# One attention-and-adapters kernel: the last twenty-four slots follow an order written out by hand instead of a loop

## The chip, the core and the metric

The kernel runs on one core of one Trainium2 chip. The core has engines that each work through their own queue in order: TensorE (PE, matmuls, with its weight loads shown apart as PEld), VectorE (DVE), ScalarE (ACT), GpSimd (POOL), and SyncE (SP), which here only issues DMAs. An engine waits on semaphores that others raise, so one late instruction holds up all that stands behind it in its queue. The metric is the device time of one execution in microseconds (us), as the median of several runs.

## The reference

Two stages follow each other. The first is attention with keys and values made from a pooled map (`kv` is averaged over 4 x 4 blocks and multiplied by `w_sr`); the second routes each row to two of eight small adapters.

```python
# B, N, C = 4, 12288, 128; 768 pooled keys a batch
kv_flat = kv_pool.reshape(B, -1, C) @ w_sr        # k = v = kv_flat
s = scale * (q @ k.transpose(0, 2, 1))
a = np.exp(s - s.max(-1, keepdims=True)); a /= a.sum(-1, keepdims=True) + 1e-09
x = (a @ v).reshape(B * N, C)                     # 49152 rows
logits = x @ w_gate                               # 8 experts, the best 2 are kept
w = softmax of the two kept logits
out = x + sum over the two of w_e * ((x @ A[e]) @ B[e])   # A: 128 x 16, B: 16 x 128
```

## The kernel before

The rows are cut into 96 chunks of 512 (24 a batch). A chunk is four tiles of 128 rows. Its way through the core has these steps, each a function of the kernel; all matmuls are issued by the helper on line 68, so the profile tells them apart by their tiles:

- `scores(k, r)` for r = 0, 1, 2 (line 238): two matmuls of 512 columns into one of two PSUM tiles `sg` (pool `ps_s`), then ACT's exp into `em` (line 246). Six score matmuls and three exps a chunk.
- `attend(k, s)` for the four tiles s (line 248): six matmuls each into `acc`, of which PSUM holds one (`ps_a`). Columns 128 to 135 of the product are already the gate logits, column 136 the sum.
- `normalize` (line 256): reciprocal and multiplication on DVE, `acc` into `xn`.
- `top` (line 276): four MAX8 on DVE. `route` (line 285): four small steps on POOL that turn the two largest logits into a tanh argument and a mask. `gates` (line 310): the tanh on ACT and two more steps on POOL give the weights `gw`.
- `transposes(kx, kh)` (line 318): four transposes of one chunk's `xn` and four of an older chunk's gated values `hg` into one PSUM tile `tt_ps`, copied out by one instruction (line 334 on ACT, line 336 on DVE).
- `down` (line 342), four matmuls by A into `h_ps`; `gate` (line 347), the product with `gw` on DVE into `hg`; `up` (line 356), four matmuls by B into `d_ps`; `finish` (line 361), the addition of `xn` on DVE and the output DMA from SP.

The tiles `tt_ps`, `h_ps`, `d_ps` share a pool `ps_m` of two PSUM banks (tag `mb`). Together `sg`, `acc` and `mb` fill PSUM. Output tiles `osb` come from a pool of six (line 59). The queries are cast to bf16 by POOL's DMAs (`cast_q`, line 77) and read back transposed by SP's DMAs (`load_qT`, line 82), four chunks at a time; a one-column copy on POOL named `late` makes a cast wait for the transposed read of the group before it.

The order is the program's order: each engine gets its instructions as the Python code emits them. A loop over chunks (line 420, from chunk 4 on) emits one *slot* for each chunk k: score 0 of k, the normalisation of k-2, transposes for k-6 and k-7, score 1, `up` and `finish` of k-8, the first tile of attend k-1, `top` and `route`, score 2, `down` and `gate` of k-6, the other three tiles of attend k-1. Chunks are routed in pairs up to chunk 71 and one by one from 72 (line 269). Three slots let two chunks enter instead of one, so that the backlog shrinks from six chunks to three:

```python
can = [k for k in left if ready[k] <= t]
enter[t] = can[:2] if t in [NB * (B - 1) + 1 + i for i in (0,1,3)] else can[:1]
```

These are slots 73, 74 and 76; the second chunk's transposes are copied by ACT (line 334), and its `down` follows in the next slot. After the loop (line 500 on) the last four chunks are finished by straight code with its own helpers: single transposes copied by ACT (`fetch`, line 523), the last attention in an `sg` tile, a carried output (`carry`, line 561: ACT copies `d_ps` to SBUF; `add_there`, line 566: POOL adds `xn` there and SP sends it), and half-chunk steps at the very end (lines 573, 644, 558).

Of the kernel before, what the change touches and what calls it, by code (L numbers as in the profile page):

```python
# [20 lines left out]
def kernel(  # L21
# [85 lines left out]
    def turn_q(g, m, engine):  # L107
        if m == 0:
            qT[g] = qpool.tile([P, GT], BF16, tag="qT", name="qT")
        ps = mtile([P, S, P], name="qT_ps")  # L110
        for i in range(S):
            mm(ps[:, i], q_f[g][:, m * S + i], id_f, is_transpose=True,
               start=(i == 0), stop=(i == S - 1))
        o = qT[g][:, m * T:(m + 1) * T].rearrange("p (s t) -> p s t", s=S)
        if engine is nc.scalar:
            keep(nc.scalar.copy(o, ps))
        else:
            keep(nc.vector.tensor_copy(o, ps))
# [39 lines left out]
    def prepare(b, adder):  # L158
# [28 lines left out]
        def keys(h):  # L187
            if h == 0:
                st["kpT"] = prep.tile([P, J, P], FP32, tag="kpT", name="kpT")
                kfT[b] = per_b.tile([P, J, P], BF16, tag="kfT", name="kfT")  # L190
            kpT = st["kpT"]
            ps = mtile([P, 2, P], name="kpT_ps")
# [4 lines left out]
            for n, (r, i, c) in enumerate(parts):  # L197
                mm(ps[:, i], kvr[b, h][:, r, i, c * C:(c + 1) * C], id_f, is_transpose=True,
                   start=(n == 0), stop=(n == len(parts) - 1))
            keep(nc.vector.tensor_scalar(kpT[:, 2 * h:2 * h + 2], ps, 1.0 / 16.0, None,  # L200
# [27 lines left out]
        for h in range(3):  # L228
            for f in (keys, keys2, values) if adder is nc.vector else (keys, values, turn):
                rest.append(lambda h=h, f=f: f(h))  # L230
# [7 lines left out]
    def scores(k, r):  # L238
        b = k // NB
        if r == 0:  # L240
# [7 lines left out]
    def attend(k, s):  # L248
        b = k // NB
        if s == 0:  # L250
# [5 lines left out]
    def normalize(k):  # L256
        ri = rpool.tile([P, S], FP32, tag="rinv", name="rinv")
        keep(nc.vector.reciprocal(ri, acc[k][:, :, VC]))  # L258
        k0, m = first[k], k - first[k]
        if m == 0:  # L260
            xg[k0] = xpool.tile([P, GC, S, VC], FP32, tag="xn", name="xn")
        x = xg[k0][:, m]
# [13 lines left out]
    def top(k):  # L276
        k0, m = first[k], k - first[k]
        if m == 0:
# [4 lines left out]
    later = []  # L283

    def route(k0):
        n = size[k0] * S
        eng = nc.gpsimd if k0 > 1 else nc.vector
        lg = xg[k0].rearrange("p m s c -> p (m s) c")[:, 0:n, C:VC]
# [10 lines left out]
        keep(eng.tensor_scalar(mask, mask, 0.0, None, op0=ALU.is_ge))  # L299


        def rest():
            gates(k0, n, eng, arg, mask)

        if k0 > 3:
            later.append(rest)
        else:
            rest()

    def gates(k0, n, eng, arg, mask):  # L310
# [50 lines left out]
    def finish(k):  # L361
# [5 lines left out]
        for d in (em, acc, xn, xT, hgT, hp, hg, dp):  # L367
            d.pop(k, None)

    LA = 4  # L370

    for m in range(GC):
        turn_q(0, m, nc.scalar)
    sums, rest = prepare(0, nc.vector)
    for h in range(3):
        for item in sums[h]:
            item()
        rest[3 * h]()
        if h > 0:
            scores(2, h - 1)  # L380
        rest[3 * h + 1]()
        if h > 0:
            scores(3, h - 1)
            rest[3 * h - 1]()
        scores(0, h)
        scores(1, h)
    rest[8]()
    scores(2, 2)
    scores(3, 2)
    rest = []  # L390

    late = const.tile([P, 1], FP32)
    keep(nc.gpsimd.tensor_copy(late, q_f[1][:, GC * S - 1, 0:1]))
    for g in range(2, 4):
        cast_q(g)
    a_bf = const.tile([P, P], BF16)
    keep(nc.vector.tensor_scalar(a_bf, a_f, 0.5, None, op0=ALU.mult))
    b_bf = const.tile([P, C], BF16)
    keep(nc.vector.tensor_copy(b_bf, b_f))
    turn_q(1, 0, nc.scalar)  # L400


    att = {LA: [0], LA + 1: [1], LA + 2: [2, 3], LA + 3: [4, 5], LA + 4: [6, 7]}
    for k in range(8, NCHUNK):
        att[k + 1] = [k]
    normed = {}
    for t, ks in att.items():
        for k in ks:
            normed[k] = t + 1 if k == ks[-1] else t
    ready = {k: normed[first[k] + size[k] - 1] + 1 for k in range(NCHUNK)}  # L410
    enter, t, left = {}, LA, list(range(NCHUNK - 3))
    while left:
        can = [k for k in left if ready[k] <= t]
        enter[t] = can[:2] if t in [NB * (B - 1) + 1 + i for i in (0,1,3)] else can[:1]
        left = [k for k in left if k not in enter[t]]
        t += 1

    sums, rest = [], []
    kh, ku, kd, kdone = [], [], [], []
    for k in range(LA, NCHUNK):  # L420
        b, i = divmod(k, NB)
        ka = att.get(k, [])
        kx = enter.get(k, [])
        if k % GC == 0:
            g = k // GC
            if 2 <= g + 1 < B * NG:
                load_qT(g + 1)
        if b + 1 < B:
            i0 = 4 if b == 0 else 0
            if i == i0:  # L430
                sums, rest = prepare(b + 1, nc.gpsimd)
                sums = sum(sums, [])
            if i0 <= i < i0 + 12:
                h, j = divmod(i - i0, 4)
                load_kv(b + 1, h, j, None)

        if k % GC == 2 and 4 <= k // GC + 2 < B * NG:
            keep(nc.gpsimd.tensor_copy(late, qT[k // GC + 1][:, 0:1]))
            cast_q(k // GC + 2)

        def after_norm(kn):
            top(kn)
            if kn == first[kn] + size[kn] - 1:
                route(first[kn])

        kn = [n for n in att.get(k - 1, []) if normed[n] == k]
        if k == LA:
            for s in range(S):
                attend(0, s)
            ka = []  # L450
        scores(k, 0)
        while later:
            later.pop(0)()
        for x_ in kd:
            down(x_)
        for n in kn:
            normalize(n)
        pairs = [(kx[j] if j < len(kx) else None, kh[j] if j < len(kh) else None)
                 for j in range(max(len(kx), len(kh)))]
        for x_, h_ in pairs[:1]:  # L460
            transposes(x_, h_, nc.vector)
        for x_ in kd:
            gate(x_)
        if k + 1 in range(GC + 1, 2 * GC):
            turn_q(1, (k + 1) % GC, nc.scalar)
        scores(k, 1)
        for u_ in ku:
            up(u_)
            finish(u_)
        for a_ in ka[:-1]:  # L470
            for s in range(S):
                attend(a_, s)
            normalize(a_)
            after_norm(a_)
        if ka and len(ka) == 1:
            attend(ka[0], 0)
        for n in kn:
            after_norm(n)
        scores(k, 2)
        for x_ in kx[:1]:  # L480
            down(x_)
            gate(x_)
        kd = []
        if rest and i in ((14, 15, 16, 18, 19, 20, 21, 22, 23) if b == 0 else (11, 12, 13, 17, 18, 19, 21, 22, 23)):
            rest.pop(0)()
        for a_ in ka[-1:]:
            for s in range(1 if len(ka) == 1 else 0, S):
                if s == S - 1:
                    for x_, h_ in pairs[1:]:
                        transposes(x_, h_, nc.scalar)  # L490
                        kd = [x_] if x_ is not None else []
                attend(a_, s)
        ku = kh
        kh = kx[:1] + kdone
        kdone = kd
        if b + 1 < B and i % 2 == 0 and (8 if b == 0 else 6) <= i <= 20:
            for _ in range(4 if b == 0 and i % 4 else 3):
                sums.pop(0)()

    K = NCHUNK - 1  # L500
    assert kh == [K - 3] and ku == [K - 4], (kh, ku)

    def bank(pool):
        if pool is ps_m:
            return mtile([P, S, P], name="tail_ps")
        if pool is ps_a:
            return ps_a.tile([P, S, 256], FP32, tag="acc", name="acc")
        return ps_s.tile([P, 2, T], FP32, tag="sg", name="sg")

    def turn_x(k, pool):  # L510
        ps = bank(pool).bitcast(BF16).rearrange("p a b -> p (a b)")[:, 0:T].rearrange("p (s c) -> p s c", s=S)
        xb = xn[k].bitcast(U16)[:, :, 1::2].bitcast(BF16)
        for s in range(S):
            mm(ps[:, s], xb[:, s, 0:C], id_bf, is_transpose=True, start=(s == 0), stop=(s == S - 1))
        xT[k] = ps

    def turn_h(k, pool):
        ps = bank(pool).bitcast(BF16).rearrange("p a b -> p (a b)")[:, 0:T].rearrange("p (s c) -> p s c", s=S)
        for s in range(S):
            mm(ps[:, s], hg[k][:, s], id_bf, is_transpose=True, start=(s == 0), stop=(s == S - 1))  # L520
        hgT[k] = ps

    def fetch(which, k):
        sb = run.tile([P, S, P], BF16, tag="tt1", name="tt1")
        keep(nc.scalar.copy(sb, which[k]))
        which[k] = sb

    def tanhs():
        for rest_ in later:
            rest_()  # L530
        later.clear()

    def part(k, o, js):
        for s in range(S):
            for j in js:
                mm(o[:, s, 0:VE], em[k][:, j, s * P:(s + 1) * P], vx[k // NB][:, j],
                   start=(j == 0 and s % 2 == 0), stop=(j == J - 1 and s % 2 == 1))

    def wide(o):
# [148 lines left out]
```

## Time and profile before

| what | value |
|---|---|
| median of 5 runs | 400.67 us (399.65 to 401.01) |
| the profiled execution | 399.65 us, of which its span is 397.9 us |
| mean granted TensorE clock | 0.996 |
| PE busy | 374.2 us (94% of the span) |
| DVE, ACT, POOL busy | 324.5, 297.3, 202.0 us |
| first score matmul of chunk 72 | 292.42 us after the span's start |
| end of slot 95 (the loop) on PE | 385.38 us |
| last DVE instruction ends | 394.73 us |
| output DMA of 256 KB, issue to landing | 3.4 us median over the run |

The profile lists instructions by line, engine, operation and tiles, with `out<-in`. A record of a matmul includes its way through the array, so records overlap: what a matmul costs PE in a stream is the distance between the starts. "Idle before" is the time in which an engine waited just before an instruction, with what ended the wait.

### The profile page before, as it was taken

The page shows a single profiled execution, that of the slowest core. Times are in us where ns is not written, and L with a number is a line of the kernel's source. Part 1 is how long each engine was busy: PE and PEld are TensorE (multiplying, and loading weights), DVE is VectorE, ACT ScalarE, POOL GpSimd, SP SyncE. Part 2 cuts the span into 40 slices and gives each one's busy share as a digit, 9 for nine tenths or more (in the row PEclk, how much of TensorE's full clock was granted, in tenths as well). Part 3 has the DMA queues.
Part 4 walks back from the last instruction along what each step waited for, and adds up shares of the span by engine and source line. Part 5 has one row for each costly group of instructions (what it writes and reads, how often), then busy time and mean ns, then how long its engine had stood idle before and what let it go on. Part 6 is the DMA issues. An engine that isn't in the chain of part 4 may idle for free.

```text
span 397.9 us, 11637 instructions
## 1 busy us (share of the span) xinstructions
PE 374.2 (94%) x4515; PEld 302.3 (76%) x4589; DVE 324.5 (82%) x944; ACT 297.3 (75%) x375; POOL 202.0 (51%) x471
## 2 busy tenths in 40 slices
PE   4898899999999999999999999999999899999993
PEld 3656678788888887888878887888877688788882
DVE  2543778889898889898898888898888788888885
ACT  3389467877787787787777787786778778888873
POOL 0010159977623586876613486876614244344443
PEclk9999999999999999999999999999999999999998
DMA  8998637996588999955679999956644477464113
GB/s 291 402 248 244 157 110 207 265 251 158 130 205 227 287 235 348 186 153 132 145 167 265 243 255 276 282 139 138 150 135 106 133 187 159 135 144 123 62 74 135
DMA packets 71464, 76.47 MB, mean 192 GB/s; under 512 B 49936, under 2 KB 50704, under 8 KB 70928
## 3 DMA queue, kind: packets, MB, share of 16 engines
q1 hardware_dynamic: 70272, 63.98, 55.0%
q0 software_dynamic: 704, 11.54, 16.7%
q8 instruction: 36, 0.59, 0.6%
q10 hardware_dynamic: 432, 0.20, 0.2%
q14 instruction: 20, 0.16, 0.2%
HBM read 50.53 MB, written 36.70 MB: 219 GB/s over the span
## 4 chain that ended last, share of the span: by engine, by line
PE 81%; DVE 5%; POOL 4%; ACT 3%; DMA 3%; issue 2%; SPq 1%; ACTq 0%; DVEq 0%; POOLq 0%
PE acc L68 32%; PE sg L68 23%; PE tt_ps L68 10%; PE h_ps L68 6%; PE d_ps L68 6%; ACT em L246 2%; POOL kvr L171 2%; PE kpT_ps L68 1%; DMA qf<-in_q_dram 1%; DVE rinv L258 1%; DMA kvr<-in_kv_dram 1%; PE v_ps L68 1%; DVE xn L263 1%; SPq L98 1%; DVE tts L336 1%
## 5 line engine op out<-in xcount | busy, mean ns | idle before, releaser
L246 ACT ACTIVATE em<-sg 128x1024 f16<-128x1024 f32 x288 | 280.7, 1024 | 78.1 <-PE sg L68 59.0
L68 PE MATMUL acc<-vx,em 128*128 128x137 f16 x2280 | 167.5, 223 | 1.3 <-DVE xn L263 1.2
L68 PE MATMUL sg<-qT,kfT 128*128 128x512 bf16 x502 | 155.2, 379 | 3.1 <-ACT em L246 2.6
L68 PEld LDWEIGHTS <-em 128*128 128x128 f16 x2304 | 145.4, 98 | 3.2 <-DVE xn L263 2.2
L68 PEld LDWEIGHTS <-tts 128*128 128x128 bf16 x740 | 56.4, 98 | 46.1 <-issue 2.8
L263 DVE TENSOR_TENSOR xn<-acc,rinv 128x544 f32<-128x544 f32 x95 | 68.8, 724 | 3.4
L293 POOL TENSOR_TENSOR over<-xn,srt 128x64 f32<-128x64 f32 (+1 forms) x116 | 30.3, 282 | 80.0 <-DVE srt L281 80.0
L350 DVE TENSOR_TENSOR hg<-h_ps,gw 128x512 bf16<-128x512 f32 x93 | 64.3, 691 | 7.4 <-PE h_ps L68 0.2
L171 POOL TENSOR_TENSOR kvr<-kvr 128x512 f32<-128x512 f32 x54 | 67.3, 1270 | 0.0
L336 DVE COPY tts<-tt_ps 128x1024 bf16<-128x1024 bf16 (+1 forms) x90 | 62.0, 689 | 1.7 <-PE tt_ps L68 0.9
L363 DVE TENSOR_TENSOR osb<-d_ps,xn 128x512 f32<-128x512 f32 x91 | 62.6, 691 | 0.6 <-PE d_ps L68 0.6
L68 PEld LDWEIGHTS <-kfT 128*128 128x128 bf16 x576 | 45.8, 98 | 6.7 <-issue 4.3
L314 POOL TENSOR_TENSOR gw<-th,over 128x64 f32<-128x64 f32 (+1 forms) x58 | 16.9, 292 | 66.6 <-ACT th L312 66.3
L258 DVE RECIPROCAL rinv<-acc 128x4 f32<-128x4 f32 x95 | 17.4, 183 | 35.4 <-PE acc L68 35.1
L68 PEld LDWEIGHTS <-xn 128*128 128x128 bf16 x384 | 29.1, 98 | 20.9 <-DVE xn L263 0.4
L68 PE MATMUL h_ps<-a_bf,tts 128*128 128x128 bf16 x372 | 36.0, 219 | 2.0 <-ACT tts L334 0.7
L68 PE MATMUL d_ps<-b_bf,tts 128*128 128x128 bf16 x364 | 35.2, 219 | 2.7 <-DVE tts L336 1.1
L68 PE MATMUL tt_ps<-id_bf,xn 128*128 128x128 bf16 x372 | 35.9, 219 | 1.2
L68 PE MATMUL tt_ps<-id_bf,hg 128*128 128x128 bf16 x368 | 35.6, 219 | 0.3 <-DVE hg L350 0.3
L281 DVE MAX8 srt<-xn 128x8 f32<-128x8 f32 x380 | 34.2, 153 | 0.2
L68 PEld LDWEIGHTS <-hg 128*128 128x128 bf16 x384 | 25.6, 98 | 1.3 <-DVE hg L350 0.5
L299 POOL TENSOR_SCALAR over<-over 128x64 f32<-128x64 f32 (+1 forms) x58 | 19.4, 335 | 5.2
(82 smaller groups left out, 201.4 us busy)
## 6 DMA issues: line engine op xcount, KB each, us to landing
out_dram<-osb SPq DMA_DIRECT2D x94, 256.0 KB, 3.4
kvr<-in_kv_dram SPq DMA_DIRECT2D x36, 512.0 KB, 6.1
qbf<-in_q_dram POOLq DMA_DIRECT2D x22, 512.0 KB, 6.0
kvr<-in_kv_dram SPq DMA_DIRECT2D x24, 256.0 KB, 5.4
qf<-in_q_dram SPq DMA_DIRECT2D x1, 1024.0 KB, 5.1
qf<-in_q_dram SPq DMA_DIRECT2D x4, 256.0 KB, 5.2
out_dram<-osb SPq DMA_DIRECT2D x3, 128.0 KB, 2.3
qT<-qbf SPq DMA_TRANSPOSE x22, 5.1
```

Of the source, the lines that this page charges most:

```text
L68: return keep(nc.tensor.matmul(*a, **k))
L171: keep(adder.tensor_tensor(u[:, lo:hi], u[:, lo:hi], v[:, lo:hi], op=ALU.add))
L246: keep(nc.scalar.activation(em[k][:, 2 * r:2 * r + 2], ps, AF.Exp, bias=0.0, scale=scale))
L258: keep(nc.vector.reciprocal(ri, acc[k][:, :, VC]))
L263: keep(nc.vector.tensor_tensor(x, acc[k][:, :, 0:VC], ri.unsqueeze(2).broadcast_to([P, S, VC]), op=ALU.mult))
L281: keep(nc.vector.max(srt[k0][:, m, s], xn[k][:, s, C:VC]))
L293: keep(eng.tensor_tensor(d, lg, so[:, :, i].unsqueeze(2).broadcast_to([P, n, 8]), op=ALU.subtract))
L299: keep(eng.tensor_scalar(mask, mask, 0.0, None, op0=ALU.is_ge))
L314: keep(eng.tensor_tensor(w[:, 0:n], th, mask, op=ALU.mult))
L336: keep(nc.vector.tensor_copy(sb[:, lo:hi], ps[:, lo:hi]))
L350: keep(nc.vector.tensor_tensor(hg[k].rearrange("p s (e r) -> p (s e) r", e=E), hp[k].rearrange("p s (e r) -> p (s e) r", e=E), gw[k0][:, m ...
L363: keep(nc.vector.tensor_tensor(osb, dp[k], xn[k][:, :, 0:C], op=ALU.add))
```

## The change

The loop and the straight code behind it are gone. Every step of the kernel gets a short name, and a function `follow` runs a text of such names in order. For the chunks before 72 the texts say what the loop did. For chunks 72 to 95 and the ending, one text of 594 items gives every step explicitly; there the steps of a chunk no longer have fixed distances from each other.

The names: `sc k r` scores, `at k s` attend, `nm` normalize, `tp` top, `ro` route, `ga` gates, `tt x h V` joint transposes copied by DVE; `xt k` four transposes of `xn` alone into a bank of a given pool, `cx k V/A` their copy by DVE or ACT; `ht k lo hi` transposes of `hg` alone, `ch k lo hi V/A` their copy; `dn2` down, `ge2 k lo hi` gate, `up2 k lo hi` up (each with pairs of tiles where lo and hi say so); `af k lo hi SP/ACT` the addition on DVE and the output DMA from the named queue; `ca k` and `pd k` the carried output by ACT and POOL; `lastroute`, `lt`, `lg_` the routing on DVE with its tanh on ACT; `pt 95 lo hi` the last attention in two parts; `lq` and `cq` the transposed read and the cast of a group of queries; `hb`, `db`, `o95` only name a PSUM tile that a later step writes.

In this text 13 chunks' transposes stay joint, 17 `xn` transposes stand alone (10 copied by DVE, 7 by ACT); 18 outputs are carried through ACT and POOL (2 before); six chunks (75, 80, 82, 88, 91, 95) are routed on DVE (only 95 of these before); scores run up to seven chunks ahead of their attention (`sc 94 0` stands before `at 88 3`). Two of the middle's output DMAs and two of the last three are issued from ACT's queue. The number of matmuls is the same.

```diff
@@ normalize: xn tiles hold the four chunks of a group, not those routed together
-        if m == 0:
-            xg[k0] = xpool.tile([P, GC, S, VC], FP32, tag="xn", name="xn")
-        x = xg[k0][:, m]
+        if k // GC not in xg:
+            xg[k // GC] = xpool.tile([P, GC, S, VC], FP32, tag="xn", name="xn")
+        x = xg[k // GC][:, k % GC]
@@ new helpers (cut)
+    def fetch_x(k, engine):
+        sb = run.tile([P, S, P], BF16, tag="tt1", name="tt1")
+        copy(engine, four(sb), xT[k])
+        xT[k] = sb
+    def fetch_h(k, lo=0, hi=S, engine="A"):
+        if lo == 0:
+            hgT[k] = run.tile([P, S, P], BF16, tag="tt1", name="tt1")
+        copy(engine, part(four(hgT[k]), lo, hi), part(hps[k], lo, hi))
+    def gate_part(k, lo, hi):
+        ...
+        keep(nc.vector.tensor_tensor(
+            part(four(hg[k]).rearrange("p a b (e r) -> p a (b e) r", e=E), lo, hi),
+            part(four(hp[k]).rearrange("p a b (e r) -> p a (b e) r", e=E), lo, hi),
+            part(g4, lo, hi).unsqueeze(3).broadcast_to([P, (hi - lo) // 2, 2 * E, RK]), op=ALU.mult))
+    def add_here(k, lo, hi, queue="SP"):
+        osb = opool.tile([P, S, C], FP32, tag="osb", name="osb")[:, 0:hi - lo]
+        keep(nc.vector.tensor_tensor(osb.rearrange("p (a b) c -> p a b c", b=2),
+                                     part(four(dp[k]), lo, hi),
+                                     part(four(xn[k][:, :, 0:C]), lo, hi), op=ALU.add))
+        keep((nc.sync if queue == "SP" else nc.scalar).dma_start(dest(k)[:, lo:hi], osb))
+    def carry(k):
+        osb = opool.tile([P, S, C], FP32, tag="osb", name="osb")
+        keep(nc.scalar.copy(four(osb), four(dp[k])))
+        dp[k] = osb
+    def add_there(k):
+        keep(nc.gpsimd.tensor_tensor(dp[k], dp[k], xn[k][:, :, 0:C], op=ALU.add))
+        keep(nc.sync.dma_start(dest(k), dp[k]))
@@ the loop over chunks becomes texts
-    for k in range(LA, NCHUNK):
-        ...
+    for k in range(14, 72):
+        follow(slot(k))
+    follow("""
+ga 68; sc 72 0; hb 75 mb; sc 73 0; xt 66 mb; db 72 mb; db 66 sg; db 64 mb; nm 70; lq 19; hb 65 mb;
+ht 65 0 4; at 71 2; db 65 sg; db 67 mb; at 71 3; sc 72 2; cx 66 V; dn2 66 mb; sc 72 1; at 71 1; ch
...
+ge2 71 0 4; nm 74; pd 66; sc 75 2; tt 72 71 V; sc 79 0; tt 73 70
+V; db 71 sg; sc 76 1; at 75 3; ga 72; up2 69 0 4; sc 77 1; at 75 0; tp 74; at 75 2; af 69 0 4 SP; ro
+73; up2 68 0 4; dn2 72 mb; db 70 mb; ca 68; ge2 72 0 4; db 74 mb; at 75 1; ga 73; nm 75; sc 76 2; cq
+21; ro 74; dn2 73 mb; tt 74 72 V; sc 78 1; ga 74; at 76 1; at 76 2; dn2 74 mb; up2 71 0 2; up2 71 2
+4; at 76 0; ge2 73 0 4; ca 71; hb 73 mb; sc 77 2; at 76 3; hb 83 mb; lastroute 75; up2 70 0 4; sc 78
+2; ge2 74 0 4; nm 76; tt 75 74 V; lt 75; sc 78 0; tp 76; ro 76; pd 68; af 70 0 4 SP; at 77 1; ga 76;
+at 77 2; at 77 3; lg_ 75; dn2 75 sg; up2 72 0 4; at 77 0; ca 72; ge2 75 0 4; sc 80 0; xt 76 mb; nm
+77; cx 76 V; sc 79 1; db 75 mb; tp 77; ht 75 0 2; ht 75 2 4; at 78 1; ht 73 0 2; ht 73 2 4; ch 75 0
+4 V; sc 81 0; ro 77; ch 73 0 4 V; up2 74 0 4; ...
+... cq 23; lg_ 82; ge2 82 0 4; tp 83; up2 80 0 2; ... pd 76; lq 23; cx 83 V; sc 86 1; ...
+... lt 91; ge2 90 0 4; db 94 mb; at 92 0; sc 95 0; ...
+2; pt 95 0 4; dn2 93 mb; ge2 92 0 4; nm 94; pt 95 4 6; up2 91 0 2; up2 91 2 4; ht 92 0 4; xt 94 mb;
+ro 93; ga 93; tp 94; ge2 93 0 2; nm 95; ca 91; pd 86; cx 94 A; xt 95 sg; ht 93 0 2; ch 92 0 4 V; ro
+94; pd 91; ga 94; lastroute 95; cx 95; up2 92 0 4; lt 95; dn2 95 sg; ge2 93 2 4; ht 93 2 4; ca 92;
+lg_ 95; pd 92; dn2 94 mb; ge2 95 0 4; ge2 94 0 4; ch 93 0 4 A; ht 95 0 4; ch 95 0 2 A; up2 93 0 4;
+ch 95 2 4 V; ht 94 0 2; ht 94 2 4; af 93 0 4 SP; ch 94 0 2 A; ch 94 2 4 A; up2 95 0 4; up2 94 0 4;
+af 95 0 4 ACT; af 94 0 2 ACT; af 94 2 4 SP
+""")
```

## The prediction

> **What bounds the kernel now.** I read the busy shares first, then TensorE's own waits by stretch, then its timeline in the last 106 us, where the change lies.
>
> ```profile
> PE 374.2 (94%) x4515; PEld 302.3 (76%) x4589; DVE 324.5 (82%) x944; ACT 297.3 (75%) x375; POOL 202.0 (51%) x471
> ...
> PEclk9999999999999999999999999999999999999998
> ```
>
> TensorE is busy almost everywhere, at its full granted clock. The table by stretch (the columns are the stretch, its length, then busy time of PE, PEld, DVE, ACT, POOL with instruction counts, clock, DMA share, GB/s) shows where it is not:
>
> ```profile
> core 0: us, PE busy (x) PEld busy (x) DVE busy (x) ACT busy (x) POOL busy (x), PEclk, DMA share, GB/s
> 292.42:296.04 3.62, 3.57 (x48) 2.91 (x47) 3.16 (x9) 2.93 (x4) 1.01 (x4) 1.00 0.84 215
> 296.04:323.19 27.15, 24.80 (x318) 19.80 (x321) 21.98 (x59) 21.28 (x29) 10.03 (x38) 1.00 0.56 138
> 323.19:385.38 62.19, 61.38 (x776) 49.92 (x787) 54.34 (x154) 51.09 (x69) 26.40 (x106) 1.00 0.45 122
> 385.38:397.90 12.52, 6.39 (x87) 5.03 (x84) 7.53 (x26) 5.55 (x14) 4.68 (x11) 0.86 0.32 117
> ```
>
> The first row is slot 72, the second slots 73 to 78 (two chunks enter in three of them), the third slots 79 to 95, the fourth the straight code at the end. PE has holes in the second and the fourth. The timeline of PE (start, record length, tile, count, idle before) gives the steps and the holes:
>
> ```profile
> 381.76 0.59 PE L68 MATMUL sg<-qT,kfT 128*128 128x512 bf16 x2
> 382.19 0.39 PE L68 MATMUL tt_ps<-id_bf,xn 128*128 128x128 bf16 x4
> 382.41 0.39 PE L68 MATMUL tt_ps<-id_bf,hg 128*128 128x128 bf16 x4
> ...
> 383.29 0.52 PE L68 MATMUL acc<-vx,em 128*128 128x137 f16 x6
> 383.65 0.59 PE L68 MATMUL sg<-qT,kfT 128*128 128x512 bf16 x2
> ...
> 390.08 0.40 PE L68 MATMUL sg<-a_bf,tt 128*128 128x128 bf16 x4 [0.51 <-ACT tt L525]
> 390.69 0.40 PE L68 MATMUL sg<-b_bf,tt 128*128 128x128 bf16 x4 [0.21 <-ACT tt L525]
> ...
> 391.80 0.27 PE L68 MATMUL tail_ps<-id_bf,hg 128*128 128x128 bf16 x2 [0.52 <-ACT tt L644]
> ...
> 394.00 0.27 PE L68 MATMUL tail_ps<-b_bf,tt 128*128 128x128 bf16 x2 [0.81 <-DVE osb L558]
> ```
>
> From start to start: a score costs 0.43 us (382.19 - 381.76), four transposes, downs or ups 0.22, an attended tile 0.36. A slot of steady work, 378.13 to 381.76, is 3.63. The holes of the second stretch are these waits (engine and line, releaser: total, times, longest; a record that reaches past the next start hides some 0.16 of each):
>
> ```profile
> PE d_ps L68 <- DVE tts L336: 1.1, 3, 0.4
> PE h_ps L68 <- ACT tts L334: 0.7, 2, 0.5
> PE d_ps L68 <- DVE hg L350: 0.2, 1, 0.2
> ```
>
> **What is lost now.** From slot 72's first score PE still has 24 slots of 3.63, and what the backlog adds: 27 sets of four at 0.2225 (six chunks' transposes, downs, seven turned `hg`, eight ups) and one chunk's 24 attention matmuls at 0.06. That is 87.1 + 6.0 + 1.4 = 94.5 us. Its last matmul ends at 394.27, 101.85 after 292.42: 7.3 us are lost. Slots 73 to 79 (to 327.33) take 31.3 for 7 x 3.63 + 12 x 0.2225 = 28.1 of work: 3.2 lost. The end takes 8.9 for 4.8 of work: 4.1 lost. No loss lies in slots 80 to 95.
>
> **The change, part by part.** *Before slot 72:* order and waits are the same on every engine, except that the `xn` tiles now hold groups of four; chunks 0 to 19 then fit the five tiles, and a tile comes free when four chunks are done instead of two. Nothing waits for `xn` there in the profile, so 0.
>
> *PE's work:* the same matmuls, so the 94.5 stay. Only holes can be gained or lost.
>
> *Work moved between engines, from slot 72 on,* in distances between starts (exp 0.915; copy of 512 on ACT 0.55, DVE 0.38 from the rows 586 and 416 ns; DVE `xn` 0.66, joint copy 0.65, 512-wide product or addition 0.63, MAX8 0.12): DVE 86.2 us (89.9 by the same prices before), ACT 85.2 (77.6), POOL 57.7 (46.7). All are below 94.5, ACT by 10%. The 16 more carried outputs cost ACT 16 x 0.55 = 8.8 and POOL 16 x 1.24 = 19.8, and take 16 x 0.63 = 10.1 from DVE. The four-dimensional gates and additions have no row; they have the 512 or 256 elements of rows at 0.69 and 0.42, which I use.
>
> The carried addition is where a rule speaks against the change: the Trainium skill, "GPSIMD Engine Reference", section "4.1 Engine selection", wants two-input additions on VectorE, as GpSimd is about 2x slower. The rows agree on the price (1.264 against 0.69), but not on the consequence: by the rule 16 moves lose some 9 us of engine time, by the stretches POOL is busy only 36.4 of 89.3 us and is not what PE waits for.
>
> *The middle, slots 72 to 95.* Places in the list are given as the us of PE work ahead of them, counted from slot 72's first score. For each wait of PE I take the PE work that the list puts between the trigger and the waiting step, and subtract what the other engines need (0.21 from a PE start to its reader, the prices above, 0.10 a hand-over, both as in the timeline). The same count on the kernel before finds its three 0.5 us waits. In the list 18 of 198 waits before the last attention come out short, and 25 more have under 0.1 to spare. The worst: after `sc 75 2` (ends 16.49 after 292.42) come three exps and three tanhs 3.11, POOL's gates of 72, 73, 74 and routes of 73, 74 at 0.54 and 0.87 with the cast of group 21 between them (0.79) 4.15, then DVE from `ge2 74` to the copy `ch 75` 6.15; with 0.21 to ACT and seven hand-overs of 0.10 `up2 74`, whose bank that copy frees, can start at 30.81, PE is there at 30.38: 0.42 lost. Three others, at 14.5, 68.6 and 84.6, lose 0.13, 0.10 and 0.23. Sum 0.9. It is at least the 0.4 of the worst. At most, POOL's small steps cost as much as its 64-wide rows, 0.07 more; some 30 stand on such chains: 0.9 + 2.1 = 3.0. I take 1.2, near the sum, as the 32-wide rows are the very shape, with 0.3 more for the other tight waits.
>
> *Queues passed.* `lq 22` stands on SP behind `cq 22`'s landing, and outputs of 72 and 78 behind it; six `osb` tiles hold that. The tightest query read: `cq 23` at 52, its landing 5.6, the read 4.8 (medians): ready at 62.6, `sc 92 0` needs it at 64.9. So 0. The DMAs on ACT's queue wait for a DVE addition, and exps wait behind them; that is in the count.
>
> *The end.* Up to `pt 95 4 6` nothing waits (91.6). Then the walk through the list, in us after 292.42: DVE finishes `nm 95` at 92.9, PE turns it to 93.2, ACT (behind `ga 94`) copies to 93.96, `dn2 95` from 94.1, `ge2 95` 94.6 to 95.3. POOL, after `pd 91`, routes 94, adds `pd 92` (1.24) and gives the weights of 94 at 95.2, so `ge2 94` ends 95.9, `ht 94` starts 96.0, two half copies on ACT end 97.1, `up2 94` ends 97.35. DVE adds 95 from 97.1 and the halves of 94 from 97.75 and 98.1: the last ends at 98.5. Before, it ended at 394.73 - 292.42 = 102.3. With POOL's dearer steps 99.5, with hand-overs of 0.05 some 98.0. What follows, 397.9 - 394.73 = 3.2, is again one half output from SP.
>
> *Sum.* 292.4 + 98.5 + 1.2 + 3.2 = 395.3 against the span 397.9: 2.6 us less. The profiled execution took 399.65, 1.0 under the median of 400.67; from the median the forecast is 398.1. Best case (0.4, 98.0): 396.8. Worst (3.0, 99.5): 400.9.
>
> Another rule would leave nothing to gain: "TensorE: Matmul & The Clock Gate", section "Back-to-back issue gap", gives about 81 ns for a matmul of 128 columns and 131 for 512 in a stream with weight loads. By it the rest would be an estimated 1092 x 0.081 + 144 x 0.131 = 107 us, more than the 101.85 that passed, and I would forecast no change. The rows say 56 and 216 ns (what the section gives for isolated matmuls), so the holes are real.
>
> **The rivals.** *ACT becomes late in the middle* (half the gain, 399.5): 85.2 of 94.5 us, one exp late holds one of two score banks; each of the two output DMAs in its queue can hold the exps for one addition, 0.69, so 1.4 in all. Against it: the tightest exps in the count miss by 0.1.
>
> *The holes only move* (no change, 400.7): the 43 short or tight waits each lose 0.06 more, as rows of one kind differ, and 2.6 are gone. For it: 93 of 198 have under 0.3 to spare (46 of 182 before). Against it: a wait shifts all later steps, so losses do not all add.
>
> *POOL's additions block the routing* (slower): each `pd` holds POOL 1.27 in front of routes that the gates wait for. Where one falls wholly into such a chain, 1.27 is lost; three more than I count give 3.8 and 401.9; from 2.7 (2.6 + 0.8 us) it is slower. For it: two stand in the last walk. Against it: POOL idles 37 of 94.5 us.
>
> *The chances.* 0.60 for the sum, 0.18 for late ACT, 0.11 each for no change and slower. What a measurement can tell from no change is 0.2%, 0.8 us: faster 0.78, same 0.11, slower 0.11. The range goes from the best case to the no-change case's lower part, 396.8 to 400.2; that of the likeliest alone is 396.8 to 399.4.
>
> **What would show it.** Right: the first score of chunk 72 still starts near 292.4; PE's waits up to the last attention total 0.4 to 3 us, none over 0.5; the last DVE instruction ends 2 to 3 us earlier and DVE `osb` after PE ends the chain. Late ACT shows as PE `sg` waiting for ACT `em`; blocked routing as DVE `hg` waiting for POOL `gw`. I am wrong if the list's copies and gates cost more than the rows of equal size, or if many tight waits each add.

## The result and the profile after

The changed kernel takes 401.41 us (median of 22 runs, 400.52 to 402.21) against 400.72 for the kernel before (42 runs, 399.65 to 401.35). The ratio is 1.0018, with a 95% interval of 1.0013 to 1.0024: a small loss where a gain of 2.6 us was forecast. The profiled execution of the changed kernel took 402.02, 0.6 above its median, with a span of 400.2.

Its busy shares, answering to those of before:

```profile
PE 373.2 (93%) x4515; PEld 301.2 (75%) x4589; DVE 322.9 (81%) x974; ACT 305.0 (76%) x389; POOL 214.3 (54%) x457
```

ACT and POOL do more, as the carried outputs ask, and PE's clock is full as before. Then the table by stretch, with stretches of the same lengths (the last one up to the end of the span), counted from slot 72's first score (columns: stretch, length, busy time of PE, PEld, DVE, ACT, POOL, clock, DMA share, GB/s):

```profile
core 0: us, PE busy (x) PEld busy (x) DVE busy (x) ACT busy (x) POOL busy (x), PEclk, DMA share, GB/s
293.90:297.52 3.62, 3.57 (x43) 2.67 (x42) 2.33 (x6) 3.15 (x5) 1.01 (x4) 1.00 0.82 169
297.52:324.67 27.15, 26.62 (x348) 21.84 (x352) 22.84 (x78) 25.09 (x35) 14.57 (x41) 1.00 0.49 112
324.67:386.86 62.19, 58.66 (x746) 47.62 (x756) 51.23 (x169) 55.44 (x80) 32.30 (x87) 1.00 0.47 127
386.86:400.20 13.34, 6.69 (x95) 5.36 (x91) 8.95 (x28) 4.80 (x13) 6.22 (x14) 0.86 0.37 139
```

The second row gained what was hoped for: PE is idle 0.53 us in it, before 2.35. The third row, which had no loss before (0.81 idle), is now idle for 3.53. The chunk order is what the forecast wanted, but something new happens there. PE's waits name it (total us, times, longest):

```profile
PE tail_ps L68 <- DVE hg L439: 3.1, 3, 1.3
PE acc L68 <- DVE xn L268: 0.4, 1, 0.4
PE sg L68 <- DVE hg L439: 0.4, 1, 0.4
PE sg L68 <- DVE xn L268: 0.4, 1, 0.4
PE sg L68 <- ACT tt L396: 0.3, 1, 0.3
PE tt_ps L68 <- DVE hg L439: 0.3, 1, 0.3
PE sg L68 <- DVE tt L396: 0.2, 1, 0.2
```

The longest stands at 338.40 (1.30 us); another of 1.16 stands at 380.34. Both wait for a gated `hg` from DVE. What DVE did ahead of the first of them (start, length, line, operation):

```profile
335.11 1.08 DVE L478 TENSOR_TENSOR both<-so 128x4 f32<-128x4 f32 x1
336.22 1.23 DVE L480 SCALAR_TENSOR_TENSOR arg<-xn,both 128x32 f32<-128x32 f32 x1
337.37 0.18 DVE L483 TENSOR_TENSOR mk<-xn,so 128x32 f32<-128x32 f32 x1
337.47 0.28 DVE L396 COPY tt<-tail_ps 128x256 bf16<-128x256 bf16 x1
337.67 0.68 DVE L439 TENSOR_TENSOR hg<-tail_ps,gw 128x512 bf16<-128x512 f32 x1
```

and POOL at the same time:

```profile
334.89 2.50 POOL L468 TENSOR_TENSOR osb<-osb,xn 128x512 f32<-128x512 f32 x2
```

The three lines 478, 480 and 483 are the small steps of `lastroute 80`. Elsewhere they take 0.17, 0.19 and 0.18 us; here a sum of four numbers takes 1.08 and the next step 1.23, and each ends within 0.1 of the end of one of POOL's two carried additions (some 336.15 and 337.39). For chunk 91 the same, at the second long wait:

```profile
377.04 0.17 DVE L478 TENSOR_TENSOR both<-so 128x4 f32<-128x4 f32 x1
377.24 1.22 DVE L480 SCALAR_TENSOR_TENSOR arg<-xn,both 128x32 f32<-128x32 f32 x1
378.38 1.30 DVE L483 TENSOR_TENSOR mk<-xn,so 128x32 f32<-128x32 f32 x1
```

with additions at 377.14 on POOL (2.49 for two). Chunks 82 (`both` 0.78) and 95 (`both` 0.89) lose less, 75 and 88 nothing. Over the short lengths that is 1.95 + 0.61 + 2.15 + 0.72 = 5.4 us in which DVE stood still. What these steps have in common is two inputs in SBUF; the products and additions of DVE that read one input from PSUM (`xn`, `hg`, `osb`) keep their 0.72, 0.69 and 0.69 us beside POOL. In its last 106 us the kernel before has these steps only for chunk 95, where `both` took 0.27 beside the last 0.26 us of an addition.

From slot 72's first score to the end of the span the kernel before took 105.48, the changed one 106.30: 0.8 more, as the medians say (0.7). That slot 72 starts at 293.90 instead of 292.42 in the profiles comes from the first 60 us, where PE waits for the load of `w_sr` 6.2 us instead of 5.0 and for `kpT` 1.0 more: no step there was changed, and the first score of 72 lies between 293.06 and 293.90 in this and all profiles below. The profiled execution of before lies 1.1 under its median and that of the changed kernel 0.6 above its own, so the 1.48 alone says little.

### The profile page after: what moved, and what is told of

It reads as the page before. It is cut to its first block, busy times and chain, and to the rows that moved or that the text cites. A ratio compares the mean times of both kernels' runs of the same rounds, so it can differ in the third digit from the quotient of the medians.

```text
span 400.2 us, 11662 instructions
## 1 busy us (share of the span) xinstructions
PE 373.2 (93%) x4515; PEld 301.2 (75%) x4589; DVE 322.9 (81%) x974; ACT 305.0 (76%) x389; POOL 214.3 (54%) x457
## 4 chain that ended last, share of the span: by engine, by line
PE 76%; DVE 9%; POOL 4%; DMA 4%; ACT 2%; issue 2%; SPq 1%; DVEq 0%; ACTq 0%; POOLq 0%
PE acc L68 30%; PE sg L68 23%; PE tt_ps L68 8%; PE d_ps L68 4%; PE h_ps L68 4%; PE tail_ps L68 4%; ACT em L252 2%; POOL kvr L171 2%; DVE hg L439 2%; DVE xn L268 1%; PE kpT_ps L68 1%; DMA w_sr_sb<-in_w_sr_dram 1%; SPq L98 1%; DMA kvr<-in_kv_dram 1%; PE v_ps L68 1%
## 5 line engine op out<-in xcount | busy, mean ns | idle before, releaser
L299 POOL TENSOR_TENSOR over<-xn,srt 128x64 f32<-128x64 f32 (+1 forms) x106 | 28.0, 285 | 87.2 <-DVE srt L286 87.1
L68 PEld LDWEIGHTS <-tts 128*128 128x128 bf16 x628 | 47.2, 98 | 32.1
L335 DVE COPY tts<-tt_ps 128x1024 bf16<-128x1024 bf16 (+1 forms) x79 | 54.3, 688 | 1.3 <-PE tt_ps L68 1.3
L349 DVE TENSOR_TENSOR hg<-h_ps,gw 128x512 bf16<-128x512 f32 x66 | 45.6, 691 | 5.1 <-PE h_ps L68 0.2
L362 DVE TENSOR_TENSOR osb<-d_ps,xn 128x512 f32<-128x512 f32 x64 | 44.3, 692 | 0.6 <-PE d_ps L68 0.6
L68 PE MATMUL tt_ps<-id_bf,xn 128*128 128x128 bf16 x316 | 30.5, 219 | 1.3 <-DVE hg L439 0.3
L68 PE MATMUL tt_ps<-id_bf,hg 128*128 128x128 bf16 x312 | 30.2, 219 | 0.3 <-DVE hg L349 0.3
L68 PE MATMUL h_ps<-a_bf,tts 128*128 128x128 bf16 x264 | 25.5, 219 | 1.0
L68 PE MATMUL d_ps<-b_bf,tts 128*128 128x128 bf16 x256 | 24.7, 219 | 0.9
L468 POOL TENSOR_TENSOR osb<-osb,xn 128x512 f32<-128x512 f32 x18 | 22.7, 1270 | 0.5 <-ACT osb L464 0.5
```

The costliest lines, as they stand in the source:

```text
L68: return keep(nc.tensor.matmul(*a, **k))
L299: keep(eng.tensor_tensor(d, lg, so[:, :, i].unsqueeze(2).broadcast_to([P, n, 8]), op=ALU.subtract))
L335: keep(nc.vector.tensor_copy(sb[:, lo:hi], ps[:, lo:hi]))
L349: keep(nc.vector.tensor_tensor(hg[k].rearrange("p s (e r) -> p (s e) r", e=E), hp[k].rearrange("p s (e r) -> p (s e) r", e=E), gw[k0][:, m ...
L362: keep(nc.vector.tensor_tensor(osb, dp[k], xn[k][:, :, 0:C], op=ALU.add))
L468: keep(nc.gpsimd.tensor_tensor(dp[k], dp[k], xn[k][:, :, 0:C], op=ALU.add))
```

## The experiments

Theory A: a GpSimd addition that reads SBUF and a VectorE step with two SBUF inputs exclude each other, so that each of DVE's small routing steps can cost a whole addition. Theory B: the many tight waits of the list add up. Theory C: the additions hold up GpSimd's own routing. Theory R came later: the additions cost through their outputs and tiles. The expectations speak of twenty carried outputs; there are eighteen. The versions were timed in three sessions, in which the kernel before took 400.51, 400.67 and 400.63 us, so differences between versions of different sessions hold to about 0.2. The edits of the list are shown item by item, without the items around them.

**Additions away, and GpSimd held without reading.** The first leaves the addition out:

```diff
     def add_there(k):
-        keep(nc.gpsimd.tensor_tensor(dp[k], dp[k], xn[k][:, :, 0:C], op=ALU.add))
         keep(nc.sync.dma_start(dest(k), dp[k]))
```

> The list as changed, without the additions of the twenty carried outputs on GpSimd (this leaves out part of the computation: those chunks lack the addition of xn; their output still goes out from the same tile). Theory A: all 5.4 us of blocked VectorE time are gone, 397.5 to 398.7. Theory B: 400.9 to 401.4. Theory C: also faster, 398 to 400, but through earlier weights from GpSimd, with the VectorE steps of unchanged length where they were slow.

The second puts work of the same length in its place:

```diff
-        keep(nc.gpsimd.tensor_tensor(dp[k], dp[k], xn[k][:, :, 0:C], op=ALU.add))
+        for i in range(FILL_N):
+            keep(nc.gpsimd.memset(fill[:, 0:FILL_W], 0.0))
+    fill = const.tile([P, 640], FP32)
+    FILL_N, FILL_W = 2, 640
```

> The list as changed, with each addition on GpSimd replaced by two fills of 640 numbers in a scratch tile, an estimated 0.62 us each by the rows of 128 numbers (204 ns) and of one (100 ns), so that GpSimd is held as long as by the addition but reads nothing from SBUF (the addition of xn is left out for those chunks). Theory A: as without the additions, 397.5 to 398.9. Theory B: 400.9 to 401.4. Theory C: as the changed kernel, 401.0 to 401.8, as GpSimd is held as long.

Measured: 397.26 without the additions (0.9918 of before, 0.9904 to 0.9931) and 397.00 with the fills (0.9912, 0.9897 to 0.9927). Two fills took 1.32 us against the addition's 1.27. In the version with fills POOL was busy beside the routing of 80 and 91 just as before, and DVE did not notice:

```profile
334.00 2.70 POOL L469 MEMSET fill<- 128x640 f32 x4
...
374.84 2.70 POOL L469 MEMSET fill<- 128x640 f32 x4
```

```profile
334.24 0.17 DVE L479 TENSOR_TENSOR both<-so 128x4 f32<-128x4 f32 x1
334.44 0.19 DVE L481 SCALAR_TENSOR_TENSOR arg<-xn,both 128x32 f32<-128x32 f32 x1
334.55 0.18 DVE L484 TENSOR_TENSOR mk<-xn,so 128x32 f32<-128x32 f32 x1
```

All 18 small steps stay at or below 0.25 us, and PE's waits of over 1 us are gone. B falls (4.4 us are gained with every tight wait in place), and so does C (GpSimd is held as long and its routes stand behind the fills as they stood behind the additions). So POOL's reading of SBUF, not its being busy, blocks the steps. The 4.4 us need not all be theirs: an output waits for its addition, but not for the fills, which write a scratch tile.

**The forms one by one.** Behind the last output, eight of each form on DVE with POOL idle, beside unbroken additions, and beside unbroken fills:

```diff
+        ("two", lambda o: V.tensor_tensor(o, wa[:, 0:n_], wb[:, 0:n_], op=ALU.add)),
+        ("stt", lambda o: V.scalar_tensor_tensor(o, wa[:, 0:n_], 2.0, wb[:, 0:n_], ...)),
+        ("psm", lambda o: V.tensor_tensor(o, pp[:, 0:n_], wb[:, 0:n_], op=ALU.add)),
+        ("imm", lambda o: V.tensor_scalar(o, wa[:, 0:n_], 2.0, None, op0=ALU.mult)),
+        ("ptr", lambda o: V.tensor_scalar(o, wa[:, 0:n_], wb[:, 0:1], None, op0=ALU.subtract)),
+        ("mx8", lambda o: V.max(o[:, 0:8], wa[:, 0:n_])),
+        ("cpy", lambda o: V.tensor_copy(o, wa[:, 0:n_])),
```

> The list as changed, with a block behind the last output that measures VectorE steps of 32 columns (and a copy of 128 from PSUM) by themselves: eight of each form with GpSimd idle, then with GpSimd doing additions of 512 numbers in SBUF without a break, then with GpSimd filling a tile (writing only). Its whole time means nothing. Theory A: the forms with two SBUF inputs take 0.13 to 0.2 us alone and 1.0 to 1.3 beside additions, the form with one input in PSUM, the search for the largest eight and the copy out of PSUM stay within 20% of their time alone, and beside fills all stay as alone. Theories B and C: every form stays within 20% in all three. Open in all: the forms with one SBUF input (copy, multiplication by a constant, subtraction of a column); the Trainium skill, SBUF - State Buffer, section Who interferes with whom, says that copies and tensor_scalar can contend too when they run in a two-port mode.

The answers by line, first beside POOL's additions (durations in ns: least, median, most; `pp` lies in PSUM, all else in SBUF):

```profile
L674 DVE TENSOR_TENSOR o_two<-wa,wb x8: 191/1138/1301, 413.7 to 419.3; 128x32 f32<-128x32 f32 x8
L675 DVE SCALAR_TENSOR_TENSOR o_stt<-wa,wb x8: 179/664/1200, 420.4 to 424.8; 128x32 f32<-128x32 f32 x8
L676 DVE TENSOR_TENSOR o_psm<-pp,wb x8: 178/191/191, 425.9 to 427.4; 128x32 f32<-128x32 f32 x8
L677 DVE TENSOR_SCALAR o_imm<-wa x8: 181/628/1124, 427.6 to 432.8; 128x32 f32<-128x32 f32 x8
L678 DVE TENSOR_SCALAR o_ptr<-wa,wb x8: 1246/1304/1305, 432.9 to 442.2; 128x32 f32<-128x32 f32 x8
L679 DVE MAX8 o_mx<-wa x8: 181/195/196, 443.4 to 445.0; 128x8 f32<-128x32 f32 x8
L680 DVE COPY o_cpy<-wa x8: 181/621/1124, 445.1 to 450.3; 128x32 f32<-128x32 f32 x8
```

and beside POOL's fills of 0.524 us each:

```profile
L674 DVE TENSOR_TENSOR o_two<-wa,wb x8: 181/192/195, 489.4 to 491.0; 128x32 f32<-128x32 f32 x8
...
L677 DVE TENSOR_SCALAR o_imm<-wa x8: 547/547/574, 494.4 to 498.5; 128x32 f32<-128x32 f32 x8
```

With POOL idle the medians are 192, 192, 191, 182, 241, 195 and 182 ns. So a two-input step pays up to a whole addition (1.3 us), the same sum with one input in PSUM pays nothing, and the search for the largest eight pays nothing. In a row some two-input steps still slip through at 0.19 us, so the median of the second form (0.66) lies below the 1.0 to 1.3 expected; that of the first (1.14) lies within. The copy out of PSUM keeps its 0.29 us. A subtraction of a column waited for a whole addition every time. Copies and multiplications by a constant also wait, and they, unlike the two-input steps, wait for fills too (0.55), as the subtraction does; there the expectation, every form beside fills as alone, failed.

This is what the Trainium skill, "SBUF — State Buffer", section "Who interferes with whom", states: GpSimd shares one pair of SBUF ports with VectorE as an exclusive lock; a VectorE step with two SBUF inputs contends with a GpSimd instruction that reads SBUF, not with one that only writes; copies and `tensor_scalar` can contend in a two-port mode; and the loser blocks fully. The rows agree with what each point makes of the lengths; the ports themselves no row shows.

**The additions moved out of the way.** The first attempt lets the addition wait for the routing mask of the chunk concerned:

```diff
+    def wait_route(k):
+        keep(nc.gpsimd.tensor_copy(late, routed[k][1][:, 0, 0:1]))
-dn2 79 mb; pd 74;
+dn2 79 mb; wl 80; pd 74;
-lastroute 82; pd 73;
+lastroute 82; wl 82; pd 73;
-pd 75; lastroute 91; lt 91;
+lastroute 91; wl 91; pd 75; lt 91;
-pd 91; ga 94; lastroute 95;
+ga 94; lastroute 95; wl 95; pd 91;
```

> The list as changed, but where an addition on GpSimd stood beside the three small VectorE routing steps of chunks 80, 82, 91 and 95, the addition now waits until those steps are done (a one-element copy of the routing mask on GpSimd, 0.18 us, stands before it; one addition of chunk 91 moves behind the gates of 94). Theory A, the two engines lock each other out: the small steps go back to 0.2 us each, 5.4 us of VectorE time come back, PE's waits for hg at line 439 fall from 3.1 us to under 1, and the time is 2.4 to 3.4 us under the changed kernel's 401.4: 398.0 to 399.0. Theory B, many short waits add up: the small steps were hidden, under 0.5 us gained, 400.9 to 401.4. Theory C, the additions hold up GpSimd's own routing: they now stand there later and before more routes, so nothing is gained or up to 1 us lost, 401.4 to 402.4.

Measured: 400.78 (1.0004, 0.9995 to 1.0013), 0.6 under the changed kernel and not the 2.4 to 3.4 expected. The 18 small steps did come back to 0.26 us or less. Two new costs took their place, both in the trace:

```profile
341.16 0.69 DVE L457 TENSOR_TENSOR osb<-tail_ps,xn 128x512 f32<-128x512 f32 x1 [2.36 <-DMA out_dram<-osb]
...
390.14 1.26 DVE L496 SCALAR_TENSOR_TENSOR gw<-th,mk 128x32 f32<-128x32 f32 x1
```

The output of 78 needs one of six `osb` tiles, and DVE stood 2.36 us until an earlier output had left it, PE 1.47. That output is the one issued at 336.59, behind the addition of 74, which now started 41.9 us after slot 72's first score instead of 41.0; it took 4.4 us to land, and 2.0 in the changed kernel. Why it took longer was not tested. And the addition of 91 now fell on another two-input step, the weights of 95 (line 496, 0.18 in the changed kernel), and PE waited 1.47 for the `hg` behind it, 0.39 in the changed kernel. There the blocking had moved, not gone.

> One place alone: the additions of 75 and 79 wait for the routing mask of 91. Theory A: arg and mk of 91 go from 2.5 us together to 0.4, PE's waits of 1.16 and 0.41 us after them go, the other blocked steps stay: 0.8 to 1.6 us under the changed kernel, 399.8 to 400.6. Theory R: no gain, 401.2 to 401.6, or a loss, as the outputs of 75 and 79 come later.

This is the edit at chunk 91 alone. Measured: 399.74 (0.9971, 0.9961 to 0.9982), 1.7 under the changed kernel's 401.4, a little more than expected. `arg` and `mk` take 0.19 and 0.18, PE's 1.16 and 0.41 us are gone, the blocked steps at 80, 82 and 95 are still 1.07 and 1.23, 0.78 and 0.90.

For chunk 80 the additions go earlier instead:

```diff
-ro 77; ch 73 0 4 V;
+ro 77; pd 72; ch 73 0 4 V;
-tp 79; ro 79;
+tp 79; ro 79; pd 74;
-dn2 79 mb; pd 74;
+dn2 79 mb;
-af 78 0 4 SP; pd 72;
+af 78 0 4 SP;
```

> One place alone, without any new wait: the additions of 72 and 74 go earlier in GpSimd's order, behind the routes of 77 and 79. Theory A: both and arg of 80 go from 2.3 us together to 0.4, PE's wait of 1.30 us at 338.4 goes, the other blocked steps stay: 0.8 to 1.6 us under the changed kernel, 399.8 to 400.6. Theory R: the outputs come earlier as well, so a gain here alone would not tell the two apart; a gain with both and arg still over 1 us would.

Measured: 401.54 (1.0014, 1.0003 to 1.0026; from 399.80 to 402.25), no gain, although the steps of 80 took 0.22 and 0.19. PE's 1.30 had gone, but 0.75 and 0.16 for ACT had come:

```profile
335.84 0.40 PE L68 MATMUL tail_ps<-a_bf,tt 128*128 128x128 bf16 x4 [0.75 <-ACT tt L396]
```

`pd` also issues the output, and the output of 72 now stood on SP in front of `lq 21`, the read of a group of queries, which was issued at 326.69 instead of 324.50. On POOL the copy that waits for this read came at 333.42 instead of 330.76, behind it the routes of 79, and on ACT the tanh of 79 stands in front of the copy that PE wants. (The profiled execution took 400.62, 0.9 under the median; what the others lost besides is not seen.) Moving the addition and leaving its output where it was tests the place in the queue:

```diff
+    def add_only(k):
+        keep(nc.gpsimd.tensor_tensor(dp[k], dp[k], xn[k][:, :, 0:C], op=ALU.add))
+    def out_only(k):
+        keep(nc.sync.dma_start(dest(k), dp[k]))
-ro 77; ch 73 0 4 V;
+ro 77; pg 72; ch 73 0 4 V;
-tp 79; ro 79;
+tp 79; ro 79; pg 74;
-dn2 79 mb; pd 74;
+dn2 79 mb; po 74;
-af 78 0 4 SP; pd 72;
+af 78 0 4 SP; po 72;
```

> The one place at chunk 80 again: the additions of 72 and 74 go earlier on GpSimd, their outputs keep their places on SP, and nothing else differs from the changed kernel. Theory A: both and arg of 80 at 0.2 us each, PE's waits at 335.8 (ACT's copy, 0.75) and 338.4 (1.30) both gone, and 0.8 to 1.6 us under the changed kernel's 401.4: 399.8 to 400.6. Theory R: as before at this place, 401.2 to 401.8.

Measured: 400.34 (0.9990, 0.9981 to 0.9998), 1.1 under the changed kernel, and both waits are gone, while those after 91 (1.16 and 0.41) stand as before. So at this place theory A was right about the additions, and theory R about the two outputs' places in SP's queue: they alone tell 401.54 from 400.34. The trace shows what the earlier output of 72 did; the share of 74's was not tested apart.

**All places at once.** Chunk 80 by the first, coupled edit, chunks 82 and 91 as in the first attempt, and at the end the additions of 91 and 92 wait for the weights of 95:

```diff
-ro 94; pd 91; ga 94; lastroute 95;
+ro 94; ga 94; lastroute 95;
-lg_ 95; pd 92;
+lg_ 95; wg 95; pd 91; pd 92;
```

> All twenty additions stay on GpSimd, each out of the way of the VectorE steps with two SBUF inputs, and without the late output tile of the first attempt: those of 72 and 74 go earlier (behind the routes of 77 and 79), those of 73, 75 and 79 wait for the routing masks of 82 and 91, those of 91 and 92 for the weights of 95. Theory A: no small step over 0.3 us, PE's waits for hg at line 439 under 0.8 us in all, and 397.0 to 398.5, near the 397.0 of the fills. Theory R, the additions cost through their outputs and tiles (the transfers that wait for them, the six osb tiles), not through VectorE: 399.5 to 401.5, with VectorE or PE waiting for a transfer of osb.

Measured: 399.19 (0.9966, 0.9953 to 0.9978), above the 398.5 expected, with PE's 0.54 for ACT's copy at 335.32 as the longest wait. With the outputs of 72 and 74 kept in place:

> As the version with all additions moved, but the outputs of 72 and 74 keep their old places in SP's order, so that the read of query group 21 no longer stands behind an addition. Theory A: every small VectorE step under 0.3 us, PE's wait of 0.54 us for ACT's copy at 335.3 goes, and 397.2 to 398.8, under the 399.19 of that version and under the kernel before. If the 2.2 us that it still lacks to the fills lie elsewhere (at the end, where the outputs of 91 and 92 now leave beside the last ones), no gain: 399.0 to 399.5.

Measured: 398.26 (0.9940, 0.9926 to 0.9953), 2.4 us under the kernel before and 3.1 under the changed one, with the same work; the places at 91 and 80 alone gave 1.7 and 1.1 of it. PE's waits from slot 72 on:

```profile
PE sg L68 <- DVE hg L439: 0.4, 1, 0.4
PE sg L68 <- DVE xn L268: 0.4, 1, 0.4
PE sg L68 <- ACT tt L396: 0.3, 1, 0.3
PE tt_ps L68 <- DVE hg L439: 0.3, 1, 0.3
PE sg L68 <- DVE tt L396: 0.2, 1, 0.2
```

Only the fourth, 0.3, lies before the last attention. This version beats both kernels. It still lacks 1.3 us to the fills, 0.9 by the profiles from slot 72 on: after its last DVE instruction (392.01) 4.29 us pass, against 3.54 with fills. Its outputs of 91 and 92 leave later, beside the last ones; that this is the reason was not tested.

**The six routings on GpSimd instead.**

```diff
-lastroute 80; ... lt 80; ... lg_ 80;
+tp 80; ro 80; ... ga 80;        (and so for 75, 82, 88, 91, 95)
```

> The six routings that the list puts on VectorE are made on GpSimd like the others (five small steps there instead of three on VectorE, weights by two steps), the additions stay where they are. Theory A: no VectorE step is blocked, PE's waits for hg after 80 and 91 shrink, but the weights now come through GpSimd behind the additions, above all those of 95 at the end (an estimated 1.2 us later by its rows of 0.45, 0.25, 0.29, 0.25 and 0.25): 398.5 to 401. If it is 402 or more, the waits for gw have taken the place of the blocked steps.

Measured: 409.22 (1.0209, 1.0195 to 1.0223), far above the range expected. DVE's waits say why:

```profile
DVE hg L439 <- POOL gw L314: 13.0, 6, 3.2
```

In the changed kernel this wait is 1.0 us in all. So the six routings must not go back to GpSimd in this list; there theory C's mechanism is real, and my 1.2 us for it was counted for one chunk alone, not for the routes behind each of them.

## Why the prediction was wrong

The step that failed is the pricing under "Work moved between engines". There the small routing steps, now for six chunks instead of one, stood in DVE's 86.2 us at their lengths alone, and the carried addition was judged by POOL's idle time: the rule against it was weighed for its price (twice VectorE's) and set aside because PE does not wait for POOL. The third rival had the additions in front of POOL's own routes. None of them had POOL stop DVE. The runs put 5.4 us of blocked DVE in its place. Of the time, 3.1 us come back when the additions are moved and all work is kept (401.41 against 398.26), and 4.4 with fills (397.00), where the outputs do not wait for additions either. In the profiled stretch the forecast was 102.9 and the changed kernel took 106.30: of the 3.4 between, 2.5 lie before the last attention's end and 0.9 behind it.

Point by point, in us after slot 72's first score:

| | forecast | changed kernel | with fills | all moved, outputs kept |
|---|---|---|---|---|
| last attention ends | 91.6 + 1.2 | 95.3 | 91.9 | 91.9 |
| last DVE instruction ends | 98.5 + 1.2 | 102.65 | 98.50 | 98.66 |
| end of the span | 102.9 | 106.30 | 102.04 | 102.95 |

- *PE's work of 94.5 and its steps:* held. Without the blocked steps the last attention ends at 91.9 for 91.6 of work.
- *Holes in the middle, 0.9 by count, 1.2 taken:* 0.3 where nothing is blocked, so they were priced too high, not too low. Tight waits did not add up. In the changed kernel the middle lost 95.3 - 91.6 = 3.7.
- *The end, 98.5 - 91.6 = 6.9 from the last attention:* 6.6 and 6.75 in the two versions without blocked steps, 7.35 in the changed kernel.
- *What follows the last instruction, 3.2:* mis-sized; 3.65 in the changed kernel, 3.54 with fills, 4.29 with all moved. That this last version comes to 102.95, the forecast's 102.9, is luck: it loses 0.9 less in the middle and 1.1 more after its last instruction.
- *Before slot 72, 0:* the profiles differ by 1.48, in the first 60 us, and the fills' profile by 0.64; nothing in the change explains it.
- *Queues passed, 0:* held for the list as it is. The edits showed how narrow it was: two outputs earlier on SP cost what the edit at chunk 80 gained.
- *Late ACT:* PE waited for ACT 0.3 us in all. *Holes only move:* not the case; those of slots 73 to 78 went, and those that came stand behind blocked steps. *POOL blocks the routing:* not in this list, but at once when the routes go there.

What could have told it before: the trace of before has one addition (POOL, 388.32 to 389.59) beside a small step of `lastroute`, `both`:

```profile
389.33 0.27 DVE L606 TENSOR_TENSOR both<-so 128x4 f32<-128x4 f32 x1
```

It took 0.27 us, a step of 0.17 elsewhere, and ended when the addition ended. The sign was weak: without any additions `both` of 95 took 0.25, and ended with a small routing step of POOL (387.13 to 387.38) instead. With the skill's section on the shared ports beside it, six routings among eighteen additions should have been priced at up to two additions each.

## What to carry to other kernels

Before an addition goes to GpSimd, list VectorE's instructions with two SBUF inputs, or copies and `tensor_scalar` from SBUF, that can run beside it: a step of 0.2 us may cost the whole addition, while the forms with one input in PSUM that were seen here were free of it. Such steps can be kept and the addition moved, but an item that also issues a transfer has two places, one on its engine and one in its queue, and only the first should move. Holding an engine and reading from it are told apart by giving it work of the same length that doesn't read.

## What the runs showed of the hardware

The same sum on VectorE takes 0.19 us beside fills on GpSimd and up to 1.30 beside additions; a copy or a product with a constant takes 0.55 beside fills of 0.52. That fills block the one-input forms and not the two-input ones was not expected from the traces. POOL loses little in return: its additions took 1.32 us at most beside these steps, against 1.26 alone.
